# Another instruction order, other PSUM banks and other repeated score products for an attention and mixer kernel on one core

## The chip, the core and the metric

The kernel runs on one core of a Trainium2 chip. The core has five engines that work side by side, each through its own list of instructions: TensorE (PE, matrix products into the PSUM banks), ScalarE (ACT, exponentials and other functions), VectorE (DVE), GpSimd (POOL) and SyncE (SP, which here only issues DMA transfers). They are held in step by semaphores. The metric is the device time of one execution in microseconds (us); less is better. A time of this kernel below is the median of several executions.

## The reference

The input x has 2048 rows of 640 columns in bf16. Two branches start from its layer norm xn: an attention with 32 heads of 20 columns, and a small mixer with two hidden layers. Their product is added to x.

```
def reference(A_x, A_wqkv, A_wo, B_x, B_w1, B_w2, B_w3, B_w4):
    x = A_x
    xn = _layernorm(x, axis=-1)
    # A: qkv = xn @ wqkv; p = softmax(q k^T * Dh**-0.5) per head; s = (p v) @ wo
    s = _A_ref(xn, A_wqkv, A_wo)
    # B: h = gelu(layernorm(xn) @ w1), quarters of h shifted by 1, 1, 2, 2 rows,
    #    x1 = xn + h @ w2, x1 + gelu(layernorm(x1) @ w3) @ w4
    g = _silu(_B_ref(xn, B_w1, B_w2, B_w3, B_w4))
    return x + s * g
```

The largest part is the softmax: 32 heads x 2048 x 2048 = 134 million exponentials.

## The kernel before

**How the work is cut.** The 32 heads go in eight head groups of four. A head takes 32 of the 128 rows of PE's array, so the four heads of a group fill the array side by side. Each group is walked in four query chunks of 512 queries, and each chunk in sixteen key tiles of 128 keys. "6_1" below is head group 6, query chunk 1; groups and chunks count from 0.

**The life of a score.** The score product of one head and one key tile has 512 columns and fills one PSUM bank. Two of them, in two banks, are turned into weights by one ACT exponential of 128x1024 (L1734). Part of the key tiles is taken off ACT: there DVE makes an approximate exponential with integer arithmetic (L1756 writes the bits, then copies with added offsets are made by DVE or POOL). The weights are then multiplied with the values: the value products L1487 (weights from ACT) and L1656 (weights from DVE and POOL), each a four of matmuls into four 32-row strips of one bank, "22" wide (20 value columns, a column of ones that gives the sum of weights, and one more).

**Two forms of a score product.** `score_pair` (L1665 to L1682) can make a score product in two ways, which write the same numbers into the same bank. In row form (L1665) it is one matmul with 32 rows of the array and 128 columns, so the products of other heads can run beside it on the other rows. In column form (L1682) it is four matmuls of 128 rows and 32 columns, which together use the whole array, against a copy of the queries in which the other heads are zero. Value products, projections and the mixer's products have the shape of the column form. Which form a product takes is decided from the order alone: it is column form where no instruction beside it in PE's list is in row form.

```
if t.flex and (pe_mode or (nx is not None and (nx.mode or nx.flex))):
    t.mode, t.dur = 1, self.row_dur * t.times
```

L1534 are score products of another cut: short key widths whose results of two key tiles share a bank, used in the last chunk.

**Repeated products.** `cfg.AGAIN` (L587) names score products by head group, query chunk, key tile and head, with a number: the product is issued that many times more into the same bank. The result is the same; the repeats are only work for PE. Two kinds of matmul beside these write nothing of use: the warming ones at the start (L927 in halves of 256 columns, L919 of 512 columns) and those of `pv_fill` (L1618).

**The other work.** The head of the program loads x (L940), the weights of the first keys and queries (L1122, one load for each) and of the values, transposes x by PE (L1099), and makes the first keys, queries and values with the general projection routine `mm_tile` (L731): fours of matmuls, "512 columns" for keys, queries and the mixer's first products, "320 columns" for values and the mixer's later products. During the attention, L731 also makes the keys, queries and values of later groups and the mixer, so PE's list mixes score products, value products and L731 fours. Head group 7 ends the attention, and then the output projection and the last products with the mixer's result are left.

**What sets the order.** The kernel builds 6946 tasks (4455 for PE, 782 for ACT, 1179 for DVE, 247 for POOL, 283 for SP). `Planner.follow` reads the global order of the tasks from the string `TABLE` (from L2180): two characters name a task, and for each kind of PSUM bank or weight buffer that the task takes, one more character says which. From that come the list of every engine, which bank a score lies in, the form of each score product and, later in `plan_sync`, the semaphore waits: a task waits for what it reads, and for the release of a bank that it takes over. Nothing is decided at run time.

```
while at < len(table):
    t = tasks[len(code) * code[table[at]] + code[table[at + 1]]]
```

ACT loads its function tables seven times, at changes between exponential and other functions; it has no work but what the list gives it.

Of the kernel before, what the change touches and what calls it, by code (L numbers as in the profile page):

```python
# [477 lines left out]
class Cfg:  # L478
# [5 lines left out]
    def __init__(self, S=2048, D=640, H=32, F=1536):  # L484
# [102 lines left out]
        self.AGAIN = {(3, 1, 3, 2): 1, (3, 1, 3, 0): 1, (3, 1, 3, 1): 1, (3, 1, 10, 3): 1, (5, 1, 14, 0): 1, (6, 0, 9, 1): 1, (6, 0, 9, 2): 1, (6, 1, 8, 0): 1, (6, 1, 15, 1): 1, (7, 1, 8, 0): 2, (7, 1, 10, 3): 2, (7, 1, 11, 3): 1, (7, 1, 11, 1): 1, (7, 1, 9, 1): 1, (7, 1, 9, 2): 1, (7, 1, 14, 1): 1, (7, 1, 0, 3): 1}  # L587
# [67 lines left out]
class Gen:  # L655
# [1665 lines left out]
```

## Time and profile before

| | us |
|---|---|
| median of 3 runs | 788.16 |
| the runs | 787.79, 788.16, 793.01 |
| the profiled execution, its own time | 790.31 |
| span in its profile | 788.2 |

The profile was taken of one execution, which was not one of the three. Its time of 790.31 us holds the span of 788.2 and 2.1 us around it. Its mean granted clock of PE is 0.993 of full speed. In the profile's lines, "arena" is the kernel's one buffer in SBUF and "psum" the banks; the arrow is output from input. A row of matmuls "x25" is 25 instructions one after another; a four counts as 4. A wait in brackets names what ended it. The windows view gives, for each stretch of time, the busy time and the number of instructions of each engine, then the granted clock of PE, the DMA engines' busy share and their GB/s.

### The profile page before, as it was taken

What the parts mean: (1) busy time and instruction counts of PE and PEld (TensorE: products, weight loads), DVE (VectorE), ACT (ScalarE), POOL (GpSimd) and SP (SyncE); (2) the same over time, 40 slices, a digit from 0 to 9 for tenths busy, and PEclk for the clock granted to TensorE, in tenths of its full rate; (3) what the DMA queues carried; (4) which work ended last, traced back from release to release, by engine and by line L of the source; (5) the groups of instructions that cost most, each with busy time, mean ns of one, the idle gap of its engine ahead of it and who ended that gap; (6) DMA issues with size and microseconds to landing.
All of it is one profiled execution on the core that took longest, in us unless ns stands there. A gap on an engine that the chain in (4) does not pass through costs nothing.

```text
span 788.2 us, 28168 instructions
## 1 busy us (share of the span) xinstructions
PE 764.4 (97%) x12551; PEld 292.6 (37%) x12551; DVE 701.5 (89%) x1179; ACT 763.8 (97%) x799; POOL 442.6 (56%) x251
## 2 busy tenths in 40 slices
PE   8999999999999999999999999999998999999997
PEld 5433333324433332233433433333324333333454
DVE  8889899889999999999998989998978798987887
ACT  7899999999999999999999999999999999998995
POOL 5576546654547647565663754665454365654742
PEclk9999999999999999999999999999999999998998
DMA  6304443531123224432353121323511121123443
GB/s 177 78 16 118 113 130 76 111 73 32 28 62 64 51 36 102 82 62 66 82 109 70 34 74 38 86 62 66 128 30 39 36 69 29 20 69 85 100 134 108
DMA packets 141486, 57.94 MB, mean 74 GB/s; under 512 B 113834, under 2 KB 136566, under 8 KB 141366
## 3 DMA queue, kind: packets, MB, share of 16 engines
q1 hardware_dynamic: 141366, 56.16, 30.6%
q8 instruction: 98, 1.61, 0.8%
q14 instruction: 22, 0.18, 0.1%
HBM read 34.52 MB, written 10.33 MB: 57 GB/s over the span
## 4 chain that ended last, share of the span: by engine, by line
ACT 53%; PE 42%; DVE 3%; DMA 1%; SPq 1%; issue 0%
ACT arena L1734 49%; PE psum L731 16%; PE psum L1665 11%; PE psum L1656 7%; PE psum L1487 5%; ACT arena L1711 2%; DVE arena L1756 1%; ACT arena L2045 1%; DMA arena<-in_A_wqkv_dram 1%; PE psum L1534 1%; PE psum L1682 1%; SPq L940 0%; PE psum L1520 0%; ACT arena L2165 0%; DVE arena L1643 0%
## 5 line engine op out<-in xcount | busy, mean ns | idle before, releaser
L1734 ACT ACTIVATE arena<-psum 128x1024 bf16<-128x1024 f32 x726 | 675.4, 1072 | 11.7 <-PE psum L1665 7.6
L1641 POOL TENSOR_TENSOR arena<-arena 128x2048 int32<-128x2048 int32 x92 | 330.3, 3600 | 208.2 <-DVE arena L1643 70.2
L1756 DVE TENSOR_SCALAR arena<-psum 128x512 uint16<-128x512 f32 x532 | 345.7, 683 | 45.9 <-PE psum L1665 33.5
L731 PE MATMUL psum<-arena 128*32 128x320 bf16 (+1 forms) x5728 | 325.7, 332 | 1.1 <-DMA arena<-in_A_wqkv_dram 0.3
L1665 PE MATMUL psum<-arena 32*128 32x512 bf16 x1941 | 253.3, 385 | 13.2 <-ACT arena L1734 8.4
L1656 PE MATMUL psum<-arena 128*22 128x512 bf16 x2128 | 181.5, 385 | 0.0
L731 PEld LDWEIGHTS psum<-arena 128*32 128x32 bf16 x5728 | 134.3, 96 | 118.0 <-issue 49.0
L1665 PEld LDWEIGHTS psum<-arena 32*128 32x128 bf16 x1941 | 67.6, 91 | 237.5 <-ACT arena L1734 121.5
L1487 PE MATMUL psum<-arena 128*22 128x512 bf16 x1452 | 138.8, 383 | 0.0
L1643 DVE TENSOR_SCALAR arena<-arena 128x4096 uint16<-128x4096 uint16 (+1 forms) x124 | 133.6, 1097 | 1.9 <-PE psum L1656 1.5
L1656 PEld LDWEIGHTS psum<-arena 128*22 128x22 bf16 x2128 | 47.9, 91 | 62.1 <-issue 40.8
L1788 POOL TENSOR_TENSOR arena<-arena 128x512 bf16<-128x512 f32 x30 | 40.7, 1357 | 35.4 <-DVE arena L1643 27.2
L1487 PEld LDWEIGHTS psum<-arena 128*22 128x22 bf16 x1452 | 35.5, 90 | 45.7 <-issue 30.4
L2130 DVE CAST arena<-psum 128x512 bf16<-128x512 f32 x48 | 32.8, 684 | 5.7 <-PE psum L731 5.2
L1953 POOL TENSOR_TENSOR arena<-arena 128x640 bf16<-128x640 bf16 x12 | 16.7, 1401 | 20.6 <-DVE arena L1643 11.2
L1711 ACT ACTIVATE arena<-psum 128x2048 bf16<-128x2048 f32 x14 | 27.1, 1934 | 0.5 <-PE psum L1665 0.5
L1337 DVE CAST arena<-psum 128x512 bf16<-128x512 f32 x36 | 24.4, 684 | 1.4 <-PE psum L731 1.0
L964 DVE BATCH_NORM_STATS2 arena<-arena 128x6 f32<-128x320 bf16 x54 | 24.9, 481 | 0.8 <-DMA arena<-in_A_x_dram 0.7
L1682 PE MATMUL psum<-arena 128*32 128x512 bf16 x248 | 24.6, 386 | 0.0
L981 POOL TENSOR_SCALAR arena<-arena 128x640 bf16<-128x640 bf16 x16 | 14.0, 879 | 18.6 <-DVE arena L1643 17.6
L1775 DVE STREAM_TRANSPOSE arena<-psum 128x512 f32<-128x512 f32 x30 | 21.3, 711 | 2.4 <-PE psum L1656 2.0
L2137 ACT ACTIVATE arena<-arena 128x6144 bf16<-128x6144 bf16 x4 | 21.1, 5316 | 0.0
(146 smaller groups left out, 337.7 us busy)
## 6 DMA issues: line engine op xcount, KB each, us to landing
arena<-in_B_w_dram SPq DMA_DIRECT2D x48, 160.0 KB, 2.6
arena<-arena SPq DMA_DIRECT2D x124, 32.0 KB, 1.9
arena<-in_B_w_dram SPq DMA_DIRECT2D x4, 960.0 KB, 5.5
arena<-in_A_x_dram SPq DMA_DIRECT2D x8, 320.0 KB, 5.4
arena<-in_A_x_dram SPq DMA_DIRECT2D x16, 160.0 KB, 2.5
out_dram<-arena SPq DMA_DIRECT2D x16, 160.0 KB, 2.2
heads<-arena SPq DMA_DIRECT2D x120, 20.0 KB, 2.0
arena<-queries SPq DMA_DIRECT2D x28, 80.0 KB
```

The source lines that it names most:

```text
L731: ins = e.matmul(pb[32 * c:32 * c + 32, 0:N], lhsT(k, c), rhs(k, c), start=(k == 0), stop=(stop and k == nk - 1), tile_position=(0, 32 * c))
L1487: ins = e.matmul(pb[32 * i:32 * i + 22, 0:512], VA[:, ql, kts[i // 2], i, :], PT[:, slots[i // 2][0].slot, slots[i // 2][0].at(i % 2):slot ...
L1641: return e.tensor_tensor(dst.bitcast(I32), U[:, ub, 0:w].bitcast(I32), bass.AP(c.tensor, c.offset, [list(c.ap[0]), [0, w // 2]]), op=ALU.add)
L1643: fa if onp else lambda e, v=v, dst=dst: e.tensor_scalar(dst, U[:, ub, 0:w], EXP_B[v], None, op0=ALU.add),
L1656: ins = e.matmul(pb[32 * i:32 * i + 22, 0:512], wv, dst[:, at:at + 512].bitcast(BF16), start=first, stop=final, tile_position=(0, 32 * i))
L1665: return e.matmul(out, self.KT[32 * i:32 * i + 32, b, 128 * kt:128 * kt + 128], q, start=True, stop=True, tile_position=(32 * i, 0))
L1682: ins = e.matmul(out[32 * c:32 * c + 32, :], self.KT[:, b, 128 * kt + 32 * c:128 * kt + 32 * c + 32], self.QM[:, gb, i, :], start=True, st ...
L1711: lambda e: e.activation(self.PT[:, hp[0].slot:hp[0].slot + 2, :], self.psum[:, 512 * h0.slot:512 * h0.slot + 2048].rearrange("p (a b) -> ...
L1734: lambda e: e.activation(self.PT[:, hp.slot, :].rearrange("p (a b) -> p a b", b=512), self.banks(hs), AF.Exp, scale=cfg.scale),
L1756: T("dve", c_dve(512), lambda e, x=x, h=hd[jj]: e.tensor_scalar(U[:, ub, x:x + 512], self.bank(h.slot)[:, :], a_exp, EXP_BIAS, op0=ALU.mul ...
L1788: return e.tensor_tensor(OnT.rearrange("p (k d a) -> p a k d", k=4, a=4), Ob[:, :].rearrange("p (a k d) -> p a k d", a=4, k=4), in1, op=AL ...
L2130: T("dve", c_dve(512), lambda e, h=h, fc=fc, i=i, G=G: e.tensor_copy(G[:, i, fc, :], self.wbank(h)[:, 0:512]), reads=[wa], writes=at, name ...
```

## The change

Two constants are replaced and nothing else: the string `TABLE` and the dictionary `AGAIN`. The tasks are the same 6946, on the same engines.

```diff
@@ -584,7 +584,7 @@
-        self.AGAIN = {(3, 1, 3, 2): 1, (3, 1, 3, 0): 1, (3, 1, 3, 1): 1, (3, 1, 10, 3): 1, (5, 1, 14, 0): 1, (6, 0, 9, 1): 1, (6, 0, 9, 2): 1, (6, 1, 8, 0): 1, (6, 1, 15, 1): 1, (7, 1, 8, 0): 2, (7, 1, 10, 3): 2, (7, 1, 11, 3): 1, (7, 1, 11, 1): 1, (7, 1, 9, 1): 1, (7, 1, 9, 2): 1, (7, 1, 14, 1): 1, (7, 1, 0, 3): 1}
+        self.AGAIN = {(3, 1, 3, 2): 1, (4, 2, 7, 0): 1, (5, 0, 7, 0): 1, (5, 3, 2, 0): 1, (6, 0, 11, 3): 1, (6, 0, 11, 0): 1, (6, 0, 11, 1): 1, (6, 0, 0, 3): 1, (6, 1, 2, 2): 1, (7, 0, 9, 0): 1, (7, 0, 0, 1): 1, (7, 1, 2, 0): 1, (7, 1, 2, 1): 1, (7, 1, 4, 0): 1, (7, 1, 7, 1): 1, (7, 1, 8, 1): 1, (7, 1, 11, 2): 2, (7, 1, 11, 3): 1, (7, 1, 9, 0): 1, (7, 1, 14, 0): 1, (7, 1, 15, 1): 1, (7, 1, 0, 2): 1, (7, 1, 1, 3): 1, (7, 1, 1, 0): 1}
...
@@ -2178,112 +2178,112 @@
 TABLE = (
-    r"#}#%###&#4$Y#'#,#?#<#-$P#(#$#/#3#.#0#1#:%t#r#2#k&Y$:#)#a$Q$R#m#l#n$S#o#b#w#v#p$T#q$U$V$-#t#s#*#x#c#u$Z$[$W$X#@#y#z#A#B#C#D#E$f#d$&#~#i$##F#G#H#I#J$|(#{$]$^#K#L#"
+    r"$Y##$-#<#%#?$f$E#3#,#4#&$:#-#$#.#(#}#'%t#*#/#0#+#@#A#B#C#D#E#F&Y#1#k#G#H#a#m#l#)#I#J#K$P#n#8#o#p#b#t#r#s$Q$S$R$T#c#q$Z$U#v$[#w#u$V#x$W$X#y#6#d#z#~$%$&%*'$|($w$$"
...
```

`AGAIN` goes from 17 entries with 19 repeats to 24 entries with 25. All 112 lines of `TABLE` differ. On PE a task stands on average 2.9 places from where it stood (75 at most), on DVE 1.8, on POOL 2.8, on SP 2.7. On ACT, 757 of the 782 tasks keep their place, and the table loads stay seven; the exponentials that move change places with near neighbours. PE's list goes from 12550 matmuls to 12616: score products in row form from 1941 to 1927 matmuls, in column form from 248 to 328 (62 products to 82). All other kinds keep their numbers.

In the rows below a row is a run of equal instructions of one line of the kernel; the shape is that of the moving operand, and "x24" is 24 instructions, so six fours. The first place is the head of PE's list. L919 are warming matmuls; L731 with 512 columns are fours for the first keys and queries, with 320 columns fours for values; L1099 are transposes of x. Before:

```order
L919 MATMUL psum<-arena 32x512 x28
L731 MATMUL psum<-arena 32x512 x4
L731 MATMUL psum<-arena 32x320 x4
L731 MATMUL psum<-arena 32x512 x32
L1099 MATMUL psum<-arena 32x128 x8
```

After:

```order
L919 MATMUL psum<-arena 32x512 x20
L731 MATMUL psum<-arena 32x512 x24
L731 MATMUL psum<-arena 32x320 x4
L731 MATMUL psum<-arena 32x512 x8
L731 MATMUL psum<-arena 32x320 x8
L1099 MATMUL psum<-arena 32x128 x8
```

The first four for values stood behind one four for queries and now stands behind six, three for keys and three for queries; two more value fours follow sooner. Two of the seven last warming fours went up, ahead of one four of transposes.

At the same place in SP's list the loads of x (L940), of the weights for keys and queries (L1122) and for values (L1395) stood, before:

```order
L940 DMA arena<-in_A_x_dram 128x2x640 x4
L1122 DMA arena<-in_A_wqkv_dram 128x5x92
L940 DMA arena<-in_A_x_dram 128x2x640 x4
L1122 DMA arena<-in_A_wqkv_dram 128x5x92
L1395 DMA arena<-in_A_wqkv_dram 128x5x320
```

After:

```order
L940 DMA arena<-in_A_x_dram 128x2x640 x6
L1122 DMA arena<-in_A_wqkv_dram 128x5x92
L940 DMA arena<-in_A_x_dram 128x2x640 x2
L1122 DMA arena<-in_A_wqkv_dram 128x5x92
L1395 DMA arena<-in_A_wqkv_dram 128x5x320
```

The weights for keys are issued after six loads of x instead of four; the weights for queries and values keep their places.

The second place is in chunk 7_0 on PE, right behind the last `pv_fill` matmuls (L1618). L1665 are score products in row form, L1682 in column form, L1656 and L1487 value products. Before:

```order
L1618 MATMUL psum<-arena 22x256 x16
L1656 MATMUL psum<-arena 22x512 x4
L1665 MATMUL psum<-arena 128x512 x17
L1487 MATMUL psum<-arena 22x512 x8
L1665 MATMUL psum<-arena 128x512 x8
L1487 MATMUL psum<-arena 22x512 x4
L1682 MATMUL psum<-arena 32x512 x4
L1656 MATMUL psum<-arena 22x512 x8
L1665 MATMUL psum<-arena 128x512 x6
L1656 MATMUL psum<-arena 22x512 x8
L1487 MATMUL psum<-arena 22x512 x4
```

After:

```order
L1618 MATMUL psum<-arena 22x256 x16
L1656 MATMUL psum<-arena 22x512 x4
L1665 MATMUL psum<-arena 128x512 x15
L1656 MATMUL psum<-arena 22x512 x4
L1487 MATMUL psum<-arena 22x512 x8
L1682 MATMUL psum<-arena 32x512 x4
L1656 MATMUL psum<-arena 22x512 x4
L1665 MATMUL psum<-arena 128x512 x7
L1487 MATMUL psum<-arena 22x512 x4
L1682 MATMUL psum<-arena 32x512 x4
L1656 MATMUL psum<-arena 22x512 x8
L1665 MATMUL psum<-arena 128x512 x8
```

The first run of row-form products is two shorter, one more value four and a column-form product stand behind it, and the next run of row-form products is seven instead of eight.

The third place is on PE where chunk 6_0 passes into 6_1 (612 to 619 us in the profile before). L731 with 320 columns are fours of the mixer there. Before:

```order
L1682 MATMUL psum<-arena 32x512 x4
L1656 MATMUL psum<-arena 22x512 x4
L1487 MATMUL psum<-arena 22x512 x4
L1665 MATMUL psum<-arena 128x512 x10
L1487 MATMUL psum<-arena 22x512 x8
L1665 MATMUL psum<-arena 128x512 x12
L1656 MATMUL psum<-arena 22x512 x4
L1487 MATMUL psum<-arena 22x512 x4
L1665 MATMUL psum<-arena 128x512 x3
L731 MATMUL psum<-arena 32x320 x24
```

After:

```order
L1487 MATMUL psum<-arena 22x512 x4
L1682 MATMUL psum<-arena 32x512 x4
L1487 MATMUL psum<-arena 22x512 x4
L1665 MATMUL psum<-arena 128x512 x4
L1656 MATMUL psum<-arena 22x512 x4
L1682 MATMUL psum<-arena 32x512 x4
L1656 MATMUL psum<-arena 22x512 x4
L1682 MATMUL psum<-arena 32x512 x4
L1656 MATMUL psum<-arena 22x512 x4
L1665 MATMUL psum<-arena 128x512 x6
L1487 MATMUL psum<-arena 22x512 x4
L1682 MATMUL psum<-arena 32x512 x4
```

Single score products that stood in runs of ten and twelve in row form now partly stand alone between value products, in column form, and the mixer's fours come later.

More of the change, by code (lines that the diff above doesn't have):

```diff
@@ new lines @@
+    r"%}%~&#%l$K%x%y&&x%$A&a%u&~$&=#'/)'0&y&$&%%z&>'1'2$B$C%J$L$D%K(Y$M$j'3&h'4$l*:#$k*;$'#*<#&?'$$N$m$n&z&{'%&|&}'&''$O$o$p*H%*I&*J$*6$*7#&@&A&q%*8%&r&s&t'($*4%*3&*5"
+    r")&u&B')'*'+&v*D#*E$*F&%Q#',%R'-%[%%]%V)%a(%b%W%S%c%X%^$q%Y%d%_%e%`%L$%M%N%O%P%T%U%Z&&&&'&(&)*L$*B)*K%*A(*C'*M(&*(Q#2(R&C&+&,&-)&.&/&0&1&2'I#'J'K'L*G*=)*>(*?&&F("
+    r"&4&5&9'&:&G'M&H'N&I&J&3&K*b(*a)*e$*d#*c'*y&*|*S'*V*9*@'P('Q'R'S'T'U*f#+7(*Z&*^+8)+9%*N&D#&E&w+.#+-$+/)(P(T'.(U&p*[%*_%v&;)(S'O#5&<'B#'C+0(+1)+2(&7*Q%*R$*T#*W'D'"
@@ new lines @@
+    r"E'F:^'d)'e#:#;'f'g#=*O*P'G*U$'H*q#*t*h)*i(*j&'h'i*g+3*X$*Y%*]''6#'7'8'9':';+4(+5)+6#*r&*u&O&*v%*x'*{*w$*z)&P&Q&R&L*l)*k(+;&*m(+<'&S&T+:']('^'_+#*`'`'a+?$+>#*p(*"
+    r"o)*n&U'b+=#&M)&N'<#'='>'?+@$'@'A'V(*s&+J#+I$+K''W'X'Y'Z'[+Q&+P'+R(+E(+F)+G%+,+A&V'*}'k&W'm('n+C'+B&+^+w#+z'o'p+D)+T)+i$+l+S(+U&'q'r*~+L&+M'+N#+~#,%+%+$+h$+k,T),"
+    r"S(,U$+H+a%+d+x#,4'-7'j'l+{,3&+)+*+V+O+g(+_%+f),#$,&,5%+j('c+++b#+&+(+`&+c)&6+'+e,,+W's#'t,C$,D#+n(+o)+p&,G'u'v,F,7&,6%,8''w'x+m+X+r)+q(+s),J#,M'y''z,K%,N+}&+|',"
@@ new lines @@
+    r"$('{'|'}'~,B),A(,E#(#&+t+v'+u&,)+y)($(%,i),l,I$,H%,L&,P((&(',Q',2,h&((,R(,k,9-$$,[%,a),d-%#-&),O,+,Z&,]%,b(,e(V#,V(W,}$,W),|#,~#,X(,Y(,m(*(+(,,/(),',*,((X,n,0(x"
+    r",z%,y$,{$-;#-:'-=-,&-G(-H)-I',^'5,.-+'--%(.((/(0(-+Y(1->,:$,=),>(,;#,<&,o(2(3,?(,1,--#,r(4#(5-A&-D+Z,f%,g$,j$(6,u(7(8(9-'(-()-)#-B#,@,p-.&-/%-0&(:#,t-E-Q$,`)-P#"
+    r",_(,c(-T(q-S([+[)#(c,s-*-8&-9%(;-<#-1-U)-W$-Z-V(-Y&-X#-[(<(=-t&-s%-u)(>(?,q-O)-N(-R%-@#-?$,w-_-b,v-e,x-2(@#(A(B-C$-y&-|-K%-q(-p)-r((C(D-h(E(F-J$-L%-F.:#-z&-}.-)"
@@ new lines @@
+    r"..(.$'.'-]0Y-`./&-v-m%-l$-n).=.;'.>.%&.(-~).#(.&#-M(d&(e.+%.*$.,$(f.A'.2&-3.D-j(-i)-k((g(h(i.1%.3%.0(]#(^.B$.E.5(.4).6$(_(`(a(b&8(G(I.i/A%-w#/B&/C&-x$-c-a-g.H-{"
+    r"'.F.7.?'.@(.8%.9&.<%)$$)%-d.K-o.G)&)'.C$.R$.S()()).J.)-^+](H#(J(K-f.N.V(-4.U)#>.W'.l#.o.]%.^&.m$.p._#0>0R#0S.Q0T.s#.X(.Y).Z$.v0U0V0W.`&.a%.b%.t$.w.M.T.q(.y).r'."
+    r"u(.[/'#.j&/&$/).k%.P.I.n'.L/*.z(.O.c.d0@#/.$.|&.{$/-#/1/0.}%0A.~%0B(L(N(Z-5)M/+)/,(//#(M0C0D0E.x/%$/N&/Q/$#/()/#/O%/R/>'/?(/@$/40F$0G0H0I/F#/E$/G'/I&/H%/J%0J0K0"
@@ new lines @@
+    r"L#0M0N0O0P0)#/`(0Q0($0*(0[/_)/5/D/=)+#),/2/a&/M%/T$/L&/P)/S#/W$)-)./6)//K/]))*)0/[(/^#/V&/U%/X0Z/7/9&b(k#(l/c$/d#/e%/Y(m/t%/w0,(/s&0+)/v0-'/Z(n(o(j0?(p/g#/f$/h)"
+    r"/30X/m%/l&/o/j)/k(/n$/b/:/</;/r$02'/q#/p03&04#/8/z/}/i0^(0_/u)0`0.0/&(O)14@0a0b/{0c00'4C#4F.e0'/|/y05$06%07)/~4Z#4^4Y(4]4y'4z&4{$0d$0e0f4D%4G4|$4}#4~%0g0h0i4I(4"
+    r"J&4H'4L&4M0#010$4`#4_$4c'4K%4a)4N4d0&0%0857'56(4W&58)4X%/x4[#4b#4e-6.f09)T.g0j$0k0l0m4h4B$5>'5=(4A#4E(0n0o0p)4q0q0r0s5?#0t5$#0u0vEm5r5%$5('5')5*5.%515['5](4O5^&"
```

195 lines of the change are left out of this document (90 added, 105 removed).

## The prediction

> **What bounds the kernel now.** I read the page's first part and its costliest groups, then the windows view cut into stages, then the chain of waits at both ends, and last the short windows and the timeline around the places where ScalarE (ACT) stands still.
>
> ```profile
> span 788.2 us, 28168 instructions
> PE 764.4 (97%) x12551; PEld 292.6 (37%) x12551; DVE 701.5 (89%) x1179; ACT 763.8 (97%) x799; POOL 442.6 (56%) x251
> ...
> L1734 ACT ACTIVATE arena<-psum 128x1024 bf16<-128x1024 f32 x726 | 675.4, 1072 | 11.7 <-PE psum L1665 7.6
> ```
>
> ACT and PE read the same 97%, but a busy PE here is one of overlapping matmuls, while ACT works through 726 exponentials of 1072 ns one after another. The stages say where ACT's 24.4 us of rest lie. The columns are the stretch, its length, busy time (and instructions) of PE, PEld, DVE, ACT, POOL, the granted clock, DMA share and GB/s:
>
> ```profile
> 0.00:36.00 36.00, 31.90 (x806) 19.28 (x810) 28.84 (x103) 28.03 (x47) 18.34 (x56) 1.00 0.52 140
> 36.00:270.00 234.00, 231.52 (x3574) 83.17 (x3570) 212.25 (x347) 233.72 (x242) 135.36 (x66) 1.00 0.31 72
> 270.00:340.00 70.00, 69.25 (x947) 22.05 (x939) 68.22 (x112) 67.53 (x73) 44.17 (x20) 1.00 0.34 69
> 340.00:704.00 364.00, 354.92 (x5629) 130.97 (x5633) 325.91 (x507) 363.50 (x368) 203.05 (x89) 1.00 0.27 59
> 704.00:720.00 16.00, 15.39 (x152) 4.49 (x141) 10.36 (x14) 13.76 (x16) 10.46 (x4) 0.79 0.45 123
> 720.00:776.00 56.00, 54.60 (x1223) 28.22 (x1222) 47.77 (x82) 51.38 (x53) 28.48 (x17) 1.00 0.41 112
> 776.00:788.00 12.00, 6.81 (x252) 4.42 (x240) 8.13 (x20) 5.89 (x7) 2.76 (x2) 0.81 0.31 107
> ```
>
> ACT rests 8.0 us in the head, 0.3 us up to 270, 2.5 us up to 340, 0.5 us up to 704, 2.2 us in the sixteen us with a clock of 0.79, 4.6 us up to 776 and 6.1 us in the tail. ACT gets the same 782 activations and seven table loads after the change, in all but the same order, so only these rests can shrink, and the 598 us in the second and fourth row have 0.8 us to give. The change is worth a few us at the most; it can cost more, if ACT starts to wait where it now does not.
>
> **Part one, the head.** The chain there, and PE's own timeline (start, length, what):
>
> ```profile
> 6.73 7.53 DMA arena<-in_A_wqkv_dram
> 14.26 0.14 issue
> 14.39 2.04 PE psum L731 x36
> ...
> 34.87 0.40 PE psum L1665 x3
> 35.27 3.76 ACT arena L1734 x4
> ```
> ```profile
> 12.16 1.67 PE L919 MATMUL psum<-arena 128*32 128x512 bf16 x25
> 13.56 0.49 PE L731 MATMUL psum<-arena 128*32 128x512 bf16 x4
> 14.39 2.04 PE L731 MATMUL psum<-arena 128*32 128x320 bf16 x36 [0.34 <-DMA arena<-in_A_wqkv_dram]
> ```
>
> PE does one four of the query projection at 13.56, then stands before the first value projection (32x320) until the value weights land at 14.26. A four of 512 columns costs (13.56 - 12.16) / 25 x 4 = 0.22 us, so PE was free at 13.78 and lost 0.6 us. In the changed order six fours of keys and queries (x24) stand ahead of that value four, with one warming four more ahead of them: keys start at 13.56 + 0.22 = 13.78, the value four is reached at 13.78 + 6 x 0.22 = 15.1, after the landing. PE's work ahead of the exponential at 35.27 is the same in both orders, and the chain shows PE alone from 14.39 up to there: a gain of 0.6 us. Against it, the key weights are issued two places later on SP's queue, after six loads of x:
>
> ```profile
> 2.85 0.47 SPq L1122 DMA_DIRECT2D arena<-in_A_wqkv_dram  x1
> 3.36 2.12 SPq L940 DMA_DIRECT2D arena<-in_A_x_dram  x4
> ...
> DMA to landing us min/median/max: 5.2/6.4/7.6
> ```
>
> An issue takes 2.12 / 4 = 0.53, so they go at 2.85 + 2 x 0.53 = 3.9 instead of 2.85; with the slower landing of that line they are there at 3.9 + 7.6 = 11.5, 2.3 us ahead of their first use. That cover hides the move. If it were gone, keys would wait about as long as values do now, and nothing would be won: the term is -0.6 to 0, and I take -0.5, near the upper row, since the cover is four times the gain.
>
> **Part two, the fall of the clock at 711.8.** In windows of 4 us the clock is full from 560 to 708, then falls:
>
> ```profile
> 576.00:580.00 4.00, 3.64 (x43) 1.03 (x43) 3.99 (x7) 4.00 (x5) 2.03 (x1) 1.00 0.02 4
> 616.00:620.00 4.00, 3.73 (x47) 1.34 (x45) 3.88 (x7) 4.00 (x6) 0.00 (x0) 1.00 0.30 66
> 704.00:708.00 4.00, 3.82 (x62) 1.27 (x50) 2.43 (x5) 3.66 (x5) 3.44 (x1) 1.00 0.58 154
> 708.00:712.00 4.00, 3.58 (x28) 1.05 (x28) 3.40 (x7) 4.00 (x6) 3.81 (x3) 0.97 0.64 201
> 712.00:716.00 4.00, 4.00 (x30) 1.10 (x30) 3.32 (x2) 3.72 (x5) 1.10 (x1) 0.50 0.21 24
> ```
>
> The window ahead of the fall holds 28 matmuls, the fewest in the body; 43 and 47 did not bring it down. What is thin there are single score products on one quarter of the array (32*128), which ACT lets through two at a time:
>
> ```profile
> 706.70 1.12 PE L1665 MATMUL psum<-arena 32*128 32x512 bf16 x9
> 708.17 1.59 PE L1665 MATMUL psum<-arena 32*128 32x512 bf16 x8 [0.35 <-DVE arena L1756]
> 709.69 0.61 PE L1487 MATMUL psum<-arena 128*22 128x512 bf16 x8
> 710.23 0.81 PE L1665 MATMUL psum<-arena 32*128 32x512 bf16 x5
> 711.20 0.64 PE L1665 MATMUL psum<-arena 32*128 32x512 bf16 x3 [0.16 <-ACT arena L1734]
> ```
>
> That is 33 matmuls from 706.70 to 711.77. The half clock then shows as three waits of ACT for products that took twice their time:
>
> ```profile
> 715.09 1.02 ACT L1734 ACTIVATE arena<-psum 128x1024 bf16<-128x1024 f32 x1 [0.28 <-PE psum L1665]
> ...
> 716.93 1.02 ACT L1734 ACTIVATE arena<-psum 128x1024 bf16<-128x1024 f32 x1 [0.81 <-PE psum L1487]
> ...
> 718.76 3.77 ACT L1734 ACTIVATE arena<-psum 128x1024 bf16<-128x1024 f32 x4 [0.81 <-PE psum L1665]
> ```
>
> The price of the fall is 0.28 + 0.81 + 0.81 = 1.9 us. In the changed order the same stretch, for the same exponentials, holds 15 single products, four whole fours, one score product done in four column pieces, and seven singles: 15 + 8 + 4 + 4 + 1 + 7 = 39 plus 4 more fours close behind in place of a run of eight singles. The first 3 us stay thin (15 against 17), the next 2 us do not (24 against 16). So the thin part is about 3 us and not 5. I take the fall as gone (-1.9); the other end is 0, if 3 us suffice. The second place of that kind, 612 to 619, gets five score products in column pieces, and I expect no new fall there.
>
> The Trainium skill, "TensorE: Matmul & The Clock Gate", Part 1 on the clock gate, has the clock go to half after an idle window of about 3.4 us, with windows that run free of the kernel's start. The trace does not agree on the first: PE shows 3.58 us of 4 busy and the clock fell. By that rule no order of products between which PE never rests 3.4 us makes or removes a fall, and the sum would be without the 1.9 us.
>
> **Part three, more work on PE.** Repeated products go from 19 to 25, and products in column pieces from 62 to 82 (matmuls of L1682 from 248 to 328). A column product takes PE alone for 0.22 us, where a single runs beside three others. At most 20 x 0.22 + 6 x 0.22 = 5.7 us are added. Most of them lie in head groups 5 to 7 where PE rests:
>
> ```profile
> 560.00:580.00 20.00, 18.68 (x261) 5.91 (x257) 17.23 (x26) 20.00 (x22) 10.56 (x4) 1.00 0.31 62
> 580.00:600.00 20.00, 18.45 (x315) 7.21 (x311) 16.92 (x26) 19.97 (x14) 14.31 (x6) 1.00 0.15 29
> 600.00:620.00 20.00, 17.53 (x287) 7.30 (x287) 17.81 (x27) 19.97 (x21) 0.63 (x1) 1.00 0.16 41
> ```
>
> 5.3 us of rest on PE with ACT at 19.97 or more of 20: I cost this at 0. The rest of PE is the cover; without it ACT waits for the whole sum, so the ends are 0 and +5.7 (a gain is excluded, as the work is only added). I stay at 0, by the row with ACT at 20.00 while PE has 1.3 us to spare.
>
> **Part four, the end and the rest.** From 720 on ACT waits for PE in eight places:
>
> ```profile
> ACT arena L1734 <- PE psum L1534: 2.5, 5, 0.9
> ACT arena L1734 <- PE psum L1665: 1.8, 3, 0.8
> ```
>
> The order there swaps neighbours, one 320-column four ahead of a product or behind it; at the last 50 rows the order of activations is the same word for word, and after the last exponential one small DVE operation changes places with its neighbour. I take 0, with one longest wait (0.9) either way. The same holds for 270 to 340 (2.5 us of rest). DMA issues after the head are reordered on SP, and the 92 long additions on POOL keep their number; POOL is busy 56% and hides its part.
>
> **The sum.** The profiled run took 790.31 us, a span of 788.2 with 2.1 us around it. Head -0.5, clock -1.9, work 0, end 0: 787.9. The median of the three runs is 788.16, 2.15 below the profiled one, nearly the price of one fall. If the median runs have the fall too, they come to 788.16 - 2.4 = 785.8; if they have none, to 788.16 - 0.5 = 787.7. Five thin us are much longer than the stretch that fell at 708 to 712, so I think most runs have it, and say 786.2.
>
> **Rivals.** (1) The clock still falls, or fell in the profiled run alone: only the head counts, 787.7, from 787 to 789. For it: the first 3 us of the stretch stay thin, and the 2.15 us between the runs. (2) Slower: PE falls behind in 545 to 620, where nine products of one query chunk become column pieces. It decides once the added work passes the 5.3 us of rest in the three rows, or if waits cannot use that rest because the products stand right ahead of the exponential that needs them. With half of the 5.7 us on the path and no fall avoided: 788.16 + 2.9 = 791.1. Against it: ACT's full rows beside a PE with room. (3) More is won: half of the 2.5 + 4.6 us of waits in 270 to 340 and 720 to 776 goes as well, 786.2 - 3.5 = 782.7. Against it: neighbours swapped by one four (0.14 to 0.22 us) do not remove waits of 0.9.
>
> **How the numbers follow.** Forecast (785 to 787) 0.45, rival 1 0.27, rival 2 0.15, rival 3 0.13. The range 783.0 to 790.5 holds the forecast, all of rival 1, and the inner third of rivals 2 and 3. One per cent, about what a measurement can tell from no change, is 7.9 us: faster than 780.3 takes more than all three gains together (0.04); slower than 796 takes the whole of the added work and a second fall (0.04).
>
> **What would show it.** Head: no wait of PE for the weights' DMA after 13.5, and the exponential of 35.26 some 0.5 earlier. Clock: 1.00 in 704 to 720 and no wait of 0.81. Work: ACT still 19.97 of 20 from 540 to 620. Wrong would be a clock under 1 at a new place, or ACT's rest above 1 us in any 20 us between 40 and 700.

## The result, and the profile after

The changed kernel took 786.37 us (median of 20 executions, 785.39 to 787.27), the kernel before 791.07 us (20 executions, 787.79 to 794.70). The ratio is 0.9945, with a 95% interval of 0.9933 to 0.9958: 0.55% less time. The executions of before spread over 6.9 us, those of the changed kernel over 1.9 us. The median of before over 20 is 2.9 us above that of the three runs shown ahead of the prediction.

The profiled execution took 787.11 us. The page of its profile begins:

```profile
span 784.7 us, 28293 instructions
PE 764.9 (97%) x12617; PEld 292.8 (37%) x12617; DVE 703.0 (90%) x1179; ACT 763.5 (97%) x799; POOL 441.7 (56%) x251
...
L1734 ACT ACTIVATE arena<-psum 128x1024 bf16<-128x1024 f32 x726 | 674.8, 1076 | 8.9 <-PE psum L1665 5.4
```

The span is 3.5 us shorter and ACT's work the same, so ACT rests less. The windows view of the changed kernel, cut into the same stages as in the prediction, says where:

```profile
0.00:36.00 36.00, 31.87 (x829) 19.36 (x833) 29.96 (x105) 29.18 (x48) 19.30 (x52) 1.00 0.52 140
36.00:270.00 234.00, 232.15 (x3578) 83.17 (x3570) 212.43 (x348) 233.91 (x242) 135.30 (x70) 1.00 0.31 72
270.00:340.00 70.00, 69.36 (x964) 22.60 (x963) 67.63 (x111) 67.65 (x71) 43.90 (x21) 1.00 0.38 72
340.00:704.00 364.00, 358.58 (x5657) 131.75 (x5649) 325.40 (x506) 363.43 (x369) 202.31 (x90) 1.00 0.28 59
704.00:720.00 16.00, 14.97 (x183) 4.75 (x186) 13.14 (x17) 15.78 (x18) 11.11 (x4) 1.00 0.48 132
720.00:776.00 56.00, 54.74 (x1328) 29.41 (x1316) 48.51 (x82) 51.07 (x53) 29.81 (x18) 1.00 0.40 116
```

ACT (the fourth pair of numbers) works 1.15 us more in the head's 36 us, and 2.02 us more in 704 to 720, where the clock reads 1.00 instead of 0.79. The other stages move by 0.1 to 0.3. A time in which the granted clock of PE drops to half is called a fall below. Since the stages slide by what was won ahead of them, a second reading takes exponentials that stand at the same place in both orders, and the times at which they start (first column: the profiled run; the runs "before again" and "before, third" are described below):

| start of the exponential of group_chunk, key tile, us | 0_0 tile 4 | 0_1 tile 10 | 2_2 tile 1 | 6_0 tile 0 | 7_0 tile 14 | 7_1 tile 6 | 7_2 tile 4 | end of span |
|---|---|---|---|---|---|---|---|---|
| before | 35.26 | 61.67 | 274.41 | 605.41 | 689.55 | 718.76 | 728.48 | 788.2 |
| before again (10.2 us at half clock) | 35.28 | 61.70 | 274.44 | 605.45 | 689.59 | 719.19 | 729.40 | 789.5 |
| before, third (no fall) | 35.19 | 61.60 | 274.33 | 605.33 | 689.48 | 716.36 | 726.18 | 785.7 |
| changed | 34.06 | 60.34 | 272.70 | 603.64 | 687.88 | 714.93 | 724.72 | 784.7 |

Read as differences against the first row, the change is ahead by 1.20, 1.33, 1.71, 1.77, 1.67, 3.83, 3.76 and 3.5 us. So there are two large steps, the head and 689 to 719, a small one between 61 and 274, and 0.3 given back at the end. Against the execution of before that had no fall, the second step is gone: 689 to 716 takes 26.88 there and 27.05 in the changed kernel. From 274 to 716 that execution takes 442.03 us and the changed kernel 442.23. So apart from the falls, the late part of the change wins nothing; what it wins at full clock is won ahead of 274 us.

### The profile page after: what moved, and what is told of

Read it like the earlier page. It is cut to its first block, busy times and chain, and to the rows that moved or that the text cites. A ratio compares the mean times of both kernels' runs of the same rounds, so it can differ in the third digit from the quotient of the medians.

```text
span 784.7 us, 28293 instructions
## 1 busy us (share of the span) xinstructions
PE 764.9 (97%) x12617; PEld 292.8 (37%) x12617; DVE 703.0 (90%) x1179; ACT 763.5 (97%) x799; POOL 441.7 (56%) x251
## 4 chain that ended last, share of the span: by engine, by line
ACT 54%; PE 40%; DVE 4%; DMA 1%; SPq 1%; issue 0%; DVEq 0%
ACT arena L1734 49%; PE psum L731 15%; PE psum L1665 11%; PE psum L1656 7%; PE psum L1487 5%; ACT arena L1711 2%; ACT arena L2137 1%; ACT arena L2045 1%; DVE arena L1756 1%; DMA arena<-in_A_wqkv_dram 1%; PE psum L1682 1%; PE psum L1534 1%; SPq L940 1%; DVE arena L1643 1%; DVE arena L1910 0%; PE psum L1520 0%
## 5 line engine op out<-in xcount | busy, mean ns | idle before, releaser
L731 PE MATMUL psum<-arena 128*32 128x320 bf16 (+1 forms) x5728 | 328.7, 332 | 0.6 <-ACT arena L2137 0.3
L1665 PE MATMUL psum<-arena 32*128 32x512 bf16 x1927 | 252.7, 384 | 8.5 <-ACT arena L1734 4.8
L1656 PE MATMUL psum<-arena 128*22 128x512 bf16 x2128 | 181.9, 381 | 0.6 <-DVE arena L1775 0.3
L731 PEld LDWEIGHTS psum<-arena 128*32 128x32 bf16 x5728 | 134.8, 96 | 116.8 <-issue 45.5
L1665 PEld LDWEIGHTS psum<-arena 32*128 32x128 bf16 x1927 | 67.6, 91 | 232.0 <-ACT arena L1734 118.1
L1487 PE MATMUL psum<-arena 128*22 128x512 bf16 x1452 | 138.7, 382 | 0.0
L1656 PEld LDWEIGHTS psum<-arena 128*22 128x22 bf16 x2128 | 47.5, 90 | 62.5 <-issue 40.6
L1487 PEld LDWEIGHTS psum<-arena 128*22 128x22 bf16 x1452 | 35.7, 90 | 45.5 <-issue 30.3
L1682 PE MATMUL psum<-arena 128*32 128x512 bf16 x328 | 31.9, 381 | 0.1
L1953 POOL TENSOR_TENSOR arena<-arena 128x640 bf16<-128x640 bf16 x12 | 16.7, 1397 | 21.2 <-DVE arena L1643 11.5
L1711 ACT ACTIVATE arena<-psum 128x2048 bf16<-128x2048 f32 x14 | 27.0, 1927 | 0.7 <-PE psum L1665 0.7
L2159 DVE TENSOR_TENSOR arena<-psum,arena 128x320 bf16<-128x320 f32 x32 | 15.4, 483 | 7.4 <-PE psum L731 7.1
```

The costliest lines, as they stand in the source:

```text
L731: ins = e.matmul(pb[32 * c:32 * c + 32, 0:N], lhsT(k, c), rhs(k, c), start=(k == 0), stop=(stop and k == nk - 1), tile_position=(0, 32 * c))
L1487: ins = e.matmul(pb[32 * i:32 * i + 22, 0:512], VA[:, ql, kts[i // 2], i, :], PT[:, slots[i // 2][0].slot, slots[i // 2][0].at(i % 2):slot ...
L1656: ins = e.matmul(pb[32 * i:32 * i + 22, 0:512], wv, dst[:, at:at + 512].bitcast(BF16), start=first, stop=final, tile_position=(0, 32 * i))
L1665: return e.matmul(out, self.KT[32 * i:32 * i + 32, b, 128 * kt:128 * kt + 128], q, start=True, stop=True, tile_position=(32 * i, 0))
L1682: ins = e.matmul(out[32 * c:32 * c + 32, :], self.KT[:, b, 128 * kt + 32 * c:128 * kt + 32 * c + 32], self.QM[:, gb, i, :], start=True, st ...
L1711: lambda e: e.activation(self.PT[:, hp[0].slot:hp[0].slot + 2, :], self.psum[:, 512 * h0.slot:512 * h0.slot + 2048].rearrange("p (a b) -> ...
```

## The experiments

The tasks of both kernels are the same, so orders can be joined: `join(a, b)` below takes the tasks of a, and then those of b that a did not have. Each task keeps the banks and weight buffers that its own order gave it; where a weight buffer was not free, another one was taken (3 times in the head, 5 and 2 times in the late joins). Repeats travel with their tasks. An execution is counted as having a fall when its mean granted clock was 0.996 or less. The runs were spread over three chips, and each stood beside executions of before on its own chip.

**Before, again (e1_before, e12_before).** No edit.

> The kernel before, unchanged, so that the granted clock of each of its executions is known beside its time. Theory (thin stretches: the clock falls to half for 6.8 us where some 3.4 us of PE's list hold fewest matmuls, and chance decides at which of them): the times go with the mean clock. Executions near 788 have no fall and a mean clock of 0.997 to 0.999, those near 790 to 791 one fall and 0.993, those near 793 two falls and 0.989. Falls lie at 706 to 720 or at 612 to 619 us. Rival (the spread of 787.8 to 794.7 has another cause, such as the DMA): the clock reads the same in executions of 788 and of 793.

e1_before: median 790.21 us (788.53 to 793.51, 12 executions). Its own executions, those of before beside all the runs here, and e12_before make 101 with a clock each, on three chips:

| mean granted clock | executions | median us | from, to |
|---|---|---|---|
| 0.997 to 0.999 | 42 | 788.60 | 787.35, 789.87 |
| 0.993 to 0.996 | 26 | 790.41 | 789.04, 792.59 |
| 0.989 to 0.992 | 23 | 791.64 | 790.52, 793.53 |
| 0.986 to 0.988 | 10 | 793.88 | 792.91, 794.98 |

Time and clock go together (correlation -0.92). Half a clock for 6.83 us lowers the mean by 0.5 x 6.83 / 788 = 0.0043, so the steps of the table are about one such interval each, at 1.2 to 2.2 us. 59 of the 101 have a fall. The rival, another cause of most of the spread, is out. The count has a blind spot: one interval of 3.41 us lowers the mean by only 0.002, and the half clock at the end of the program lowers it by 0.001 to 0.003 in the traces, so an execution at 0.997 can hold a short fall. The profiled one of e11_value_later, at 0.997, does. "No fall" below means none that the mean shows. The windows view of the profiled execution of e1_before shows a longer fall than the first profile did:

```profile
708.00:712.00 4.00, 3.69 (x24) 0.98 (x24) 3.23 (x7) 4.00 (x6) 3.81 (x3) 0.80 0.45 120
712.00:716.00 4.00, 4.00 (x27) 0.97 (x30) 3.38 (x2) 3.34 (x5) 1.15 (x1) 0.50 0.22 24
716.00:720.00 4.00, 4.00 (x36) 0.98 (x32) 0.78 (x2) 2.38 (x3) 1.68 (x1) 0.50 0.22 64
720.00:724.00 4.00, 3.58 (x49) 0.89 (x49) 3.14 (x5) 3.61 (x5) 1.92 (x1) 0.92 0.52 156
```

> The kernel before once more, for one look. If this execution has no fall, the stretch from the exponential of 689.5 to that of 718.8 shows what before loses there at full clock: theory (the fall is all) 27.1 to 27.4 us; rival (the order there makes ACT wait at full clock too) 27.8 or more. If it has a fall, it settles nothing but the place: 705 to 712 or 614 to 620 us.

e12_before: one execution, 787.89 us, without a fall. The same stretch of the same kernel:

```profile
704.00:708.00 4.00, 3.74 (x58) 1.20 (x50) 2.43 (x6) 3.66 (x5) 3.52 (x1) 1.00 0.83 239
708.00:712.00 4.00, 3.65 (x28) 1.04 (x28) 3.40 (x7) 4.00 (x6) 3.81 (x3) 1.00 0.44 118
712.00:716.00 4.00, 3.81 (x50) 1.07 (x47) 3.24 (x2) 4.00 (x5) 1.24 (x2) 1.00 0.21 24
```

The window from 708 holds 28 matmuls in 4 us, as in the first profile, and the clock stays at 1.00; ACT is busy 4.00 of 4.00. So the order makes a fall possible there, and which execution gets one differs with the same instructions. From 689.48 to 716.36 it takes 26.88 us, less than the 27.1 that was expected: at full clock ACT waits only 0.2 us in this stretch, and the fall is all. It cost 29.21 - 26.88 = 2.3 us in the first profile and 29.60 - 26.88 = 2.7 in the second.

**The head alone (e2_head, e11_value_later).**

```diff
-order = before
+order = join(after[:422], before)
```

> The kernel before with the changed order up to 38 us and its own order from there on; the repeats are those of before. Theory (the head's gain arrives at the end in full): 1.2 us below the executions of before with the same number of falls, as the exponential of 35.26 us came at 34.06 in the changed kernel; the fastest near 786.6, the median near 789.9; falls as in before. The prediction's size: 0.5 us, fastest 787.3, median 790.6. Rival (the head's gain is lost in later waits): times of before, within 0.3.

Median 787.81 us (785.95 to 789.92, 12 executions), ratio 0.9976 (0.9960 to 0.9991). Its 7 executions without a fall have a median of 786.83, 18 of before beside them 788.95: 2.1 us, more than the 1.2 of the trace. Why the medians differ by more is not shown; the start of that exponential varies by itself, from 33.47 to 35.10 us in the six profiles with the changed head. 5 of 12 have a fall, and the profiled one shows it (0.68 in 704 to 720). In the trace the exponential of 35.26 us starts at 34.00, and that lead of 1.26 is still there, as 1.24, at 689 us (688.31 against 689.55). The head's gain arrives in full, and no part of the later stages is needed for it.

In the second one, the first value four is moved in PE's list of before, behind seven fours for keys and queries:

```diff
 L919 MATMUL psum<-arena 32x512 x28
-L731 MATMUL psum<-arena 32x512 x4
-L731 MATMUL psum<-arena 32x320 x4
-L731 MATMUL psum<-arena 32x512 x32
+L731 MATMUL psum<-arena 32x512 x28
+L731 MATMUL psum<-arena 32x320 x4
+L731 MATMUL psum<-arena 32x512 x8
```

> The kernel before with one four moved: the first value projection behind all seven fours for keys and queries that follow it there. The prediction's step (the wait of PE for the value weights is the gain of the head): the wait of 0.34 is gone and the exponential of 35.26 us comes 0.3 to 0.6 earlier. Rival (the 1.1 us between the first query copy and that exponential come of other parts of the head's order): below 0.2 earlier. Falls as in before.

Median 789.65 us (786.92 to 794.04, 10 executions, 7 with a fall), ratio 0.9989 (0.9963 to 1.0015): not told apart from before. The exponential starts 0.36 us earlier than in the first profile, within the expected 0.3 to 0.6. The time from PE's first key or query four to the exponential of 35.26 us tells more. It was 21.71 us in the two first profiles of before (13.56 to 35.27), 21.06 in e11 (13.84 to 34.90), but also 21.08 in e12_before (14.11 to 35.19), which has the old order and no wait for the value weights either. The reason stands in PE's timeline of e12_before:

```profile
12.22 0.38 PE L919 MATMUL psum<-arena 128*32 128x512 bf16 x1 [1.28 <-issue]
...
14.11 2.26 PE L731 MATMUL psum<-arena 128*32 128x512 bf16 x39
```

PE stood 1.28 us for nothing that the profile shows (0.67 in the first profile), came to its first value four 0.5 later, and the weights were there. e8_before_no_repeats, with the old head and no wait, took 21.17. So the wait costs 21.71 - 21.07 = 0.64 us, as the prediction had it, but only in executions where PE is early. In e11 PE stood 0.95 us at that place and was late too, so its weights would have been there in the old order as well: e11 agrees with the price, but does not test it.

Of the profiles with the changed head, e2_head, e5_after, e9_no_repeats and e7_after_thin need 20.2 us for the same piece (13.81 to 34.00 in e2_head), e4_no_repeats 20.48 and the changed kernel 20.54. In the last two the value weights landed behind the six fours; the chain of the changed kernel:

```profile
6.13 1.74 SPq L1122
7.91 7.13 DMA arena<-in_A_wqkv_dram
15.04 0.14 issue
15.17 1.02 PE psum L731 x20
...
33.67 0.40 PE psum L1665 x4
34.07 1.93 ACT arena L1734 x2
```

That leaves 21.07 - 20.19 = 0.88 us that the changed head wins without that wait. 0.22 of it is one warming four less behind PE's first key four; about 0.2 to 0.3 is a pause at 31.3 us, which all eight profiles with the old head show and none of the six with the new (PE's timeline of before):

```profile
31.63 0.59 PE L731 MATMUL psum<-arena 128*32 128x512 bf16 x8 [0.30 <-issue]
```

The last 0.4 was not traced to an instruction.

**The late order alone (e3_late, e10_late).**

```diff
-order = before
+order = join(before[:5126], after[:6590], before)
```

> The kernel before with the changed order and repeats from 564 to 743 us alone. Theory (the late order takes the falls away and does nothing else): no execution under a clock of 0.996, all times between 787.3 and 789, median 788.1, so 3.0 below the median of before. Rival (falls do not hang on the order there): median 791, spread of 7 us as before.

Median 789.99 us (789.64 to 791.70, 12 executions), ratio 1.0001 (0.9984 to 1.0019). No execution has a fall, and the spread is 2.1 us: that part came as the theory had it. But every execution lies above the 787.3 to 789 that it expected, the median by 1.9 us. The trace shows where: from 274 to 605 us this kernel takes 331.75 us where before takes 331.00, and from 728 to the end of the span 61.2 where before takes 59.7. Both places hold a joint of the two orders, where weight buffers were chosen anew. That the joints cost these 2 us was not tested by itself; the run tells of the falls, not of the late order's own time.

```diff
-order = before
+order = join(before[:6163], after)
```

> The order and repeats of before up to 689 us, where both orders have done the same tasks, and those of the change from there to the end. Theory (the stretch of 689 to 720 makes most of the falls, 612 to 619 the rest): 1 to 3 of 12 executions have a fall; from the exponential at 689.5 to that at 718.8 it takes 27.05 us as in the changed kernel; median 787.5. Rival (the falls come of 612 to 619 as much): 5 of 12 or more.

Median 789.60 us (787.75 to 791.35, 12 executions), ratio 0.9988 (0.9966 to 1.0009). 2 of 12 have a fall, within the expected 1 to 3, and in the profiled one (787.75 us) 689.29 to 716.40 takes 27.1 as expected. But the median is 2.1 above the expectation, and executions with a clock of 0.997 and 0.998 reach 791.35. A short fall would not lower the mean by more than 0.002, so some may hide there; where the time went was not seen, since only the fastest execution was profiled.

**Filling the thin stretches of before (e6_before_filled).**

```diff
-        self.PVF = {"pvd7_0_4_2": 3, "pvd7_0_4_3": 2, "pv7_0_k9": 1}
+        self.PVF = {'pvd7_0_4_2': 3, 'pvd7_0_4_3': 4, 'pv7_1_b0': 2, 'pv7_1_b2': 2, 'pvd7_1_1_2': 1, 'pvd7_1_0_2': 1, 'pvd7_1_2_0': 1, 'pvd7_1_0_0': 1, 'pv7_1_b4': 1, 'pvd7_1_1_3': 1, 'pvd7_1_1_0': 1, 'pvd7_1_3_0': 1, 'pvd6_0_4_0': 1, 'pv6_0_b4': 1, 'pv6_0_k13': 2, 'pvd6_0_4_1': 2, 'pv6_0_k9': 1}
...
-                def fnpv(e, kts=kts, slots=slots, ends=ends):
+                def fnpv(e, kts=kts, slots=slots, ends=ends, kind=kind, x=x, quad=quad, qc=qc):
```

The second line lets a fill's name mean its own product; without it a product looks up the name of the last one of the loop, which is why the old third entry did nothing.

> The kernel before, in its own order, with 21 fills (each 8 matmuls of 256 columns that add zero, 4.6 us of PE in all) in front of value products at 613 to 619 and 706 to 720 us, and the one fill named pv7_0_k9, which did nothing, taken out of the list. Counted as matmuls of 512 columns, the share of positions of a 3.41 us window with fewer than 22 goes from 0.46 to 0.03. Theory (the falls come of such windows, whatever the order): at most 1 of 12 executions has a fall, where 25 of 47 of before had one; times within 788 to 790.5. Rival (order or repeats, not the number of matmuls): falls in about half, and the fills only cost.

1 of 12 executions has a fall, where 15 of 24 of before beside it had one. The order is that of before, so added full-height work in the stretch is enough to hold the clock in nearly all executions. It does not pay: median 791.22 us (790.41 to 795.04), ratio 1.0022 (1.0004 to 1.0039), 2.8 us above the executions of before without a fall. In the trace, 1.1 us is lost from the exponential at 605 to that at 648, and the stretch that takes 26.88 us in e12_before takes 28.84. The upper bound of the expected time, 790.5, was passed: so the fills in front of products that ACT waits for were not hidden.

**The repeats (e4_no_repeats, e5_after, e9_no_repeats, e8_before_no_repeats).** The first edit is that of e4 and e9, on the changed kernel; e5_after has no edit; e8 does the same to the kernel before.

```diff
-        self.AGAIN = {(3, 1, 3, 2): 1, (4, 2, 7, 0): 1, (5, 0, 7, 0): 1, (5, 3, 2, 0): 1, (6, 0, 11, 3): 1, (6, 0, 11, 0): 1, (6, 0, 11, 1): 1, (6, 0, 0, 3): 1, (6, 1, 2, 2): 1, (7, 0, 9, 0): 1, (7, 0, 0, 1): 1, (7, 1, 2, 0): 1, (7, 1, 2, 1): 1, (7, 1, 4, 0): 1, (7, 1, 7, 1): 1, (7, 1, 8, 1): 1, (7, 1, 11, 2): 2, (7, 1, 11, 3): 1, (7, 1, 9, 0): 1, (7, 1, 14, 0): 1, (7, 1, 15, 1): 1, (7, 1, 0, 2): 1, (7, 1, 1, 3): 1, (7, 1, 1, 0): 1}
+        self.AGAIN = {}
```

> The changed kernel with its 25 repeated score products left out, the order unchanged. Theory (the order alone keeps the thin stretches full enough): the thinnest 3.4 us in PE's list go from 24 to 21 four-hundred-twelve-column matmuls, which is above or at the 21 and 18 of before; at most 2 of 10 executions have a fall, median 786.4 within 0.6. Rival (the repeats hold the clock): half of the executions or more have a fall, mean clock 0.993 or less, median 788 to 790.

(512 columns are meant.) Median 785.57 us (784.50 to 788.18, 12 executions), a little below the expected 785.8 to 787.0, ratio 0.9948 (0.9931 to 0.9964); no fall.

> The changed kernel, unchanged, as a control on the same chip as the three runs beside it. Theory: no fall in any execution (mean clock 0.997 or more), median 2.5 us below the fall-free executions of before on this chip. Rival (the chips differ in how they throttle): some executions at 0.994 or less.

Median 786.22 us (785.70 to 786.49, 7 executions), ratio 0.9948 (0.9929 to 0.9966); no fall; 2.2 below the 788.42 of the 9 executions of before without one.

> The changed kernel without its 25 repeats once more, now beside the changed kernel itself. Theory (in the changed order the repeats only cost PE time, most of it in front of exponentials of 689 to 720): 0.4 to 0.9 us below the changed kernel, no fall. Rival (the repeats are hidden, and the 0.8 us seen were the other chip): equal within 0.3 us.

Median 785.51 us (785.05 to 785.98, 6 executions), ratio 0.9942 (0.9921 to 0.9962); no fall. It is 0.71 us below e5_after on the same chip. So in the changed order the repeats hold nothing, in 18 executions without them, and cost 0.7. The windows view shows one place, first the changed kernel, then e9:

```profile
689.00:704.00 15.00, 14.08 (x240) 5.83 (x238) 13.82 (x21) 14.79 (x15) 5.54 (x4) 1.00 0.14 22
704.00:720.00 16.00, 14.97 (x183) 4.75 (x186) 13.14 (x17) 15.78 (x18) 11.11 (x4) 1.00 0.48 132
```
```profile
689.00:704.00 15.00, 13.83 (x248) 5.80 (x248) 14.25 (x22) 15.00 (x16) 5.77 (x4) 1.00 0.16 28
704.00:720.00 16.00, 13.89 (x173) 4.03 (x166) 13.27 (x17) 15.90 (x17) 10.75 (x5) 1.00 0.46 127
```

PE has 1.1 us more rest in the second row, and ACT 0.21 and 0.12 less.

> The kernel before without its 19 repeats. The share of window positions with fewer than 22 matmuls goes from 0.46 to 1.0, at three places. Theory: every execution has a fall, most two or more, mean clock 0.985 to 0.992, median 791.5 to 794. Rival (the repeats do not bear on the clock and only cost): falls in half as before, median 0.5 us below before.

Median 788.34 us (787.34 to 791.00, 12 executions), ratio 0.9980 (0.9965 to 0.9996), and 4 of 12 with a fall, where the theory wanted all 12. This contradicts the count as it was made: leaving matmuls out did not bring more falls. With so few executions, 4 of 12 is not told apart from the 15 of 24 of before beside it either, so the repeats are not shown to have done harm. What was left out are row-form products, a matmul on 32 rows each. A second count, made after these falls were known, gives those a quarter. The fewest in any 3.41 us are as follows (from the traces, between 40 and 770 us; the place in us). The fifth column lays such windows end to end and says for which share of their starting points at least one holds fewer than 12 by the second count:

| kernel | fewest, all alike | fewest, row form a quarter | executions with a fall | share of starts with a window under 12 |
|---|---|---|---|---|
| before (e12) | 20.0 (707), 21.0 (616) | 8.2 (706), 11.2 (616) | 59 of 101 | 0.50 |
| before without repeats (e8) | 18.0 (707), 19.0 (615) | 10.5 (707), 10.8 (615) | 4 of 12 | 0.92 |
| before, filled (e6) | 21.0 (708) | 8.2 (708) | 1 of 12 | 0.11 |
| changed order from 689 on (e10) | 21.0 (616), 24.0 (715) | 11.2 (616), 12.0 (715) | 2 of 12 | 0.20 |
| changed order from 564 to 743 (e3) | 24.0 (585), 24.0 (716) | 12.0 (585), 12.0 (716) | 0 of 12 | 0 |
| changed | 24.0 (583), 24.0 (714) | 12.0 (583), 12.0 (714) | 0 of 27 | 0 |
| changed without repeats (e9) | 22.0 (583), 23.0 (708) | 11.5 (583), 15.2 (713) | 0 of 18 | 0.03 |
| the same, in row form (e7, below) | 21.0 (710), 22.0 (583) | 11.5 (583), 14.2 (710) | 0 of 12 | 0.03 |

The second count fits every row but that of e8, and there it is far off: 0.92 would be 11 falls of 12, and 4 came. (The profiled execution of e8 has a fall itself; the places ahead of it alone give 0.84.) So neither count holds in all runs, and 12 is no threshold. What the runs do show is that added work (e6) and the changed late order (e3, e5) take the falls away, the latter without the repeats too (e4, e9).

**Column form back to row form (e7_after_thin).**

```diff
-                if t.flex and (pe_mode or (nx is not None and (nx.mode or nx.flex))):
+                if t.flex and (t.name in ROWS or pe_mode or (nx is not None and (nx.mode or nx.flex))):
...
+        self.AGAIN = {}
```

> The changed kernel without its repeats, and with the 32 score products behind 575 us that stand in column form put back into row form, in the changed order. Two readings of what a thin stretch is: (all) every matmul of 512 columns counts one; the share of 3.41 us positions with fewer than 22 goes from 0 to 0.26, so about 3 of 12 executions have a fall. (fours) matmuls of the full 128 rows count, and a row-form product of 32 rows a quarter; the thinnest positions stay at 11.2 to 11.5 for a share of 0.03 to 0.08, so 0 or 1 of 12. The prediction's step (column pieces and repeats help to hold the clock) is right with the first alone. Time 785.5, as without the repeats, plus or minus 0.5.

Median 788.21 us (787.28 to 790.09, 12 executions), ratio 0.9971 (0.9952 to 0.9991), and no fall in 12. That agrees with the second count (0 or 1), while the first wanted 3; it shows that the column form is not needed either. The time is not as expected: it is 2.7 us above e9 instead of equal. The two ran on different chips, but there the executions of before without a fall read 788.28 and 788.42, so the chips do not explain it. The windows of e7, then of e9:

```profile
604.00:689.00 85.00, 83.40 (x1240) 28.94 (x1235) 72.04 (x110) 84.58 (x90) 44.63 (x15) 1.00 0.17 40
689.00:720.00 31.00, 28.61 (x377) 9.53 (x369) 27.11 (x38) 30.67 (x33) 17.87 (x7) 1.00 0.31 78
```
```profile
604.00:689.00 85.00, 82.51 (x1295) 30.48 (x1291) 72.97 (x111) 85.00 (x92) 46.35 (x16) 1.00 0.18 40
689.00:720.00 31.00, 27.72 (x410) 9.82 (x410) 27.52 (x38) 30.90 (x32) 16.52 (x8) 1.00 0.31 79
```

15 and 11 of the 32 products lie in these stretches. With 55 and 33 matmuls fewer, PE is busy 0.9 us longer in each, and ACT starts to wait from 604 to 689, where it was busy 85.00 of 85. So a row-form product alone between fours costs more here than four column matmuls. By the starts of the exponentials the profiled execution, 1.1 us above the median, loses 1.4 and 0.4 us in the two stretches; another 1.5 is lost behind 716 us, where few of the products lie, and its cause is open. The Trainium skill, "TensorEngine Tiling (Array Packing)", section Key Properties, says that a change of the tiling mode drains the engine. The rows fit that: (0.9 + 0.9) us more for the products changed in these two stretches, with fewer matmuls; no row shows the drain itself.

## Why the prediction was right or wrong

**The time.** 786.2 was forecast, 786.37 came, in the range and by the likeliest case. That the two lie so close is luck: the base was too low and the gain too small by about as much. The sum started from 788.16, and the median of before over 20 executions is 791.07. The sum's gain was 2.0 to 2.4; the medians differ by 4.7 and the profiled executions by 3.2. The prediction left open whether most executions have the fall or the profiled one alone; the 101 executions say 59, many with more than one interval. Two of the three runs it started from had none by their time. Between executions without a fall the change is worth 2.2 us (e5_after), where the prediction's case without falls had 0.5. Nearly all of that lies in the head (2.1 by e2_head).

**Part one, the head: right in kind, too small.** The wait of 0.6 for the value weights is there and costs 0.64 where it occurs. The step that failed is "PE's work ahead of the exponential at 35.27 is the same in both orders", from which the chain's PE share was taken as fixed: the changed head wins another 0.88 there, 0.22 of it by one warming four less. The term of 0.5 measured 1.2 in the traces and 2.1 by the medians of e2_head. The key weights' move on SP did no harm: PE's first key four starts at 13.53, where the query four stood at 13.56. The value weights landed 0.8 later than before (15.04 against 14.26), behind the six fours and not ahead of their end as the prediction had it, which cost 0.3.

**Part two, the clock: right, with the wrong count.** The price of 1.9 us measured 2.3 in the same profile (29.21 against 26.88). By the mean clock the fall is gone in 27 of 27 executions of the changed kernel with its repeats, and 18 of 18 without; falls of 3.41 us alone are not excluded. What failed is the counting of all matmuls, with column pieces as help: e8 contradicts the count, and e9 and e7 show that repeats and pieces are not needed. What does decide is open, as neither count fits e8. (The prediction's sum of 39 also takes the product in four pieces as one matmul; by its own count it is 42.) The fours that now stand among the singles are what the two orders differ by there (PE's timeline of the changed kernel):

```profile
706.82 0.61 PE L1665 MATMUL psum<-arena 32*128 32x512 bf16 x6 [0.43 <-ACT arena L1734]
707.36 0.40 PE L1656 MATMUL psum<-arena 128*22 128x512 bf16 x4
707.58 0.60 PE L1487 MATMUL psum<-arena 128*22 128x512 bf16 x8
708.01 0.39 PE L1682 MATMUL psum<-arena 128*32 128x512 bf16 x4
708.23 0.39 PE L1656 MATMUL psum<-arena 128*22 128x512 bf16 x4
708.65 1.62 PE L1665 MATMUL psum<-arena 32*128 32x512 bf16 x7
```

Twenty matmuls of the full height stand between the two runs of singles, where before had eight. The prediction expected no new fall at 612 to 619, but did not see that before itself can fall there. The profiled execution of e11, with before's order there, shows it, with 704 to 720 at 1.00 in the same execution:

```profile
616.00:620.00 4.00, 3.73 (x41) 1.37 (x44) 3.88 (x6) 4.00 (x6) 0.00 (x0) 0.87 0.30 66
620.00:624.00 4.00, 4.00 (x58) 1.43 (x50) 0.98 (x3) 3.13 (x3) 3.43 (x1) 0.70 0.25 38
```

By the clock rule of the Trainium skill, "TensorE: Matmul & The Clock Gate", Part 1, which the prediction weighed, no order without an idle window makes a fall. The traces agree with its free-running windows of 3413 ns (half-clock intervals within the program last 3.41 us in e11, 6.83 in the first profile and 10.24 in that of e1, at other places in other executions). They do not agree that an idle window is needed: PE was busy 3.58 to 3.73 of 4 us where the falls began, and e6 removed all but one in 12 with added work alone.

**Part three, the work: the size held, the reason did not.** It was costed at 0, with 0 to +5.7 as ends "(a gain is excluded, as the work is only added)". Measured against the execution of before without a fall, the stretch from 274 to 716 takes 0.2 us longer in the changed kernel, and as much in e5_after (442.20). But this is a balance and not only PE's rest as cover. The repeats cost 0.7, and the column form saves time: 2.7 us for 32 products in e7. So the excluded gain exists. What the 20 further column products of the change are worth alone was not run. ACT stayed at 19.95 to 20.00 of 20 us from 540 to 620, where the prediction asked for 19.97.

**Part four: right within its bounds.** From 728 us to the end it takes 0.3 to 0.4 us more than before (59.9 against 59.7 and, in the third, 59.6), and the waits of ACT behind 720 in the changed kernel are of the same kind and size:

```profile
ACT arena L1734 <- PE psum L1534: 2.6, 5, 0.9
ACT arena L1734 <- PE psum L1665: 2.1, 3, 1.0
```

Between 61 and 274 us 0.4 was won, which no step had; in the waits view from 36 to 274, two waits of ACT for score products, 0.8 us together, are gone.

**The rivals.** The clock did not go on falling (787.7), PE did not fall behind in 545 to 620 (791.1), and of the waits in 270 to 340 and 720 to 776 next to nothing was won (782.7; ACT works 0.1 us more and 0.3 less there). The best kernel of the study is the changed one without its repeats: 785.51 and 785.57 us in two runs.

## What to carry to other kernels

Where times spread by several us, put each execution's granted clock beside its time before any other reason is looked for, and take the base of a forecast from many executions. A stretch in which PE is nearly always busy can still lose the clock; here these were stretches mostly of matmuls on 32 rows, and full-height work spread among them held it. How few is too few is not settled. A single product in another array shape between others can cost more than four matmuls in the same shape.

## What the runs showed of the hardware

The granted clock fell with PE busy in 3.58 of 4 us, and the same instructions ran at full clock in another execution. PE's pauses marked "issue" at 12 us differ from execution to execution of the same list (0.67, 0.70 and 1.28 us in three profiles of before; none, and 0.27, in two of the changed kernel). The exponential that starts at 34.06 us in the changed kernel's profile starts at 33.47 in e5_after, the same kernel; how much of that comes of the pauses was not separated.
